# A gated mix of two attentions on one core: unit 14 normalised later, and the output projection's loads in two tiles a block

## The chip, the cores and the metric

The kernel runs on one core of a Trainium2 chip. A core has TensorE (matmuls), VectorE, ScalarE and GpSimd, each with its own queue of instructions that it works off in order; SyncE, whose queue here issues nearly all DMAs; and 16 DMA engines. The metric is device time of one execution in microseconds, the median of several runs.

## The reference

The input x has 2048 rows of 448. Two attentions with 16 heads of 28 columns read it, each with its own weights, and a gate mixes their outputs row by row:

```
g   = sigmoid(sum(x * gate_w))
q,k,v = x @ wqkv                           # for A and for B
A:  8 keys at distances 0, 2, .. 14 behind each row, softmax, times v
B:  all 2048 keys, softmax, times v
out = g * (a @ A_wo) + (1 - g) * (b @ B_wo)
```

The kernel puts g and 1 − g on the two attention outputs ahead of the projection. The projection is then one product: 2048 rows by 896 columns (448 of A, 448 of B) with the two stacked output weights.

## The kernel before, in words

**Numbers.** The matrices that go through TensorE in the projection are split in two parts, a rounded one (hi) and the rest (lo); each product is three matmuls, hi·hi, hi·lo, lo·hi. A split is one rounding copy, usually on ScalarE, and one subtraction on VectorE or GpSimd.

**Attention B** is cut in 16 units: u = 4·g + b is the group g of four heads with the block b of 512 query rows. A unit has 16 steps, one for each 128 keys; steps are counted through, 0 to 255, and the last unit, 15, is steps 240 to 255. In a step TensorE makes four score tiles (line 980), ScalarE two exponentials of 128x1024 (line 985), and TensorE adds the weighted sum of the step before into the accumulator `av` (line 946). While unit u runs, the scores of unit u + 1 are also made once for their row maxima; in unit 15 there is nothing left of that. Attention A runs beside it on GpSimd and VectorE; when its last output is stored, `a_done` is called, in step 240 here.

**Hooks.** Other work is hung into steps: `at(pos, st, f)` puts f into the program at a place of step st. "pre" is ahead of the step's scores, "dve" and "act" after them, "end" behind the weighted sum. A hook only sets the place in the order in which each engine's queue is filled. Within its queue an instruction starts as soon as its data are there.

**Normalising a unit** after its last step, with f its following unit's first step: `fin_copy` copies the accumulator with its row of sums (ScalarE, line 850); `fin_sum` stores the sums to DRAM (855); `fin_sum2` reads them back 16 to a partition (859); `fin_inv` inverts them and multiplies by 1 − g (863, 864); `fin_spread` stores that (868); `fin_spread2` reads it back, each head's row onto 32 partitions, four DMAs (873); `fin_on` multiplies on GpSimd (879); `fin_hi` rounds on ScalarE (883); `fin_lo` subtracts on GpSimd (887); `fin_store` stores both parts to DRAM, eight DMAs. The list `l` in the main loop gives the steps, counted from f. For unit 14 f is 240.

**The output projection.** Its 16 tiles j are of 128 rows; four tiles make a block b of 512 rows. A tile is seven pieces of the 896 columns, each three matmuls (line 832): 21 matmuls of 128x448. For each block the seven pieces are loaded: `op_load_a(b, k)`, k 0 to 3, loads A's output raw (one DMA, line 802, tall 128 rows, the last 64), which `op_split` splits (line 808 for block 0 on VectorE, 810 on ScalarE for the others, and 811 on VectorE); `op_load_b(b, k)` loads B's stored hi and lo (two DMAs, line 99, the helper `dma_r`). So a block is twelve loads. The tiles of blocks b and b + 1 have separate buffers. Raw pieces, unit outputs and results share one ring of eight buffers (`mtile`).

Block 0's loads are hung into steps by `a_done`. Tile 0's first nine matmuls are in step 255 between the last two weighted sums, and the rest of it follows the last weighted sum. `op_tile(j, behind)` is one tile of the projection: while block b is multiplied, it loads and splits block b + 1. `behind` is one step of unit 15's normalising for each of tiles 0 to 6: the sum in tile 0, the store in tile 6. Then `op_out` takes the tile out of its accumulator (two accumulators in turn; even tiles on ScalarE, line 843, odd ones on VectorE, line 841) and stores it (844). In SyncE's queue a tile's loads stand behind the result of the tile before, and ahead of what `behind` issues.

Of the kernel before, what the change touches and what calls it, by code (L numbers as in the profile page):

```python
# [20 lines left out]
NU = NG * NB  # L21
# [4 lines left out]
def gated_mix_kernel(ctx: ExitStack, tc: tile.TileContext, xT, xn, gw, wA, wB, woAB, out):  # L26
    nc = tc.nc
# [70 lines left out]
    def dma_r(dst, src):  # L98
        nc.sync.dma_start(dst.bitcast(F32), src.bitcast(F32))  # L99
# [112 lines left out]
    with tc.tile_pool(name="xp", bufs=1) as xp, tc.tile_pool(name="wp", bufs=2) as wp:  # L212
# [243 lines left out]
        for n, t in enumerate(tiles):  # L456
# [4 lines left out]
            for w in splits:  # L461
                i, k = (n - splits[w][0]) * splits[w][1], splits[w][1]
# [60 lines left out]
    def at(pos, st, f):  # L523
        hooks.setdefault((st, pos), []).append(f)
# [46 lines left out]
    def mtile(name):  # L571
        return pm.tile([128, 512], F32, tag="M", name=name)
# [185 lines left out]
    OP0 = NJ * (NU - 2)  # L758
# [19 lines left out]
    def a_done(st):  # L778
        adone.append(st)
        assert st < OP0 + 24, st  # L780
        actx.close()
        oP["2"] = ctx.enter_context(tc.tile_pool(name="wop2", bufs=2))
        for k in range(4):
            at("end", st + 1 + k, lambda k=k: (op_load_a(0, k), op_load_b(0, k)))
            at("dve", st + 4 + k, lambda k=k: op_split(0, k, nc.vector.tensor_copy))

    for k in range(7):
        at("pre", WO_AT + k, lambda k=k: raw_wo(k))
# [4 lines left out]
    def oa_tiles(b):  # L793
        if b not in oaT:
            oaT[b] = [[oP["2"].tile([128, 512], F32R, tag=f"oa{p}{k}", name=f"oa{p}{k}") for p in ("hi", "lo")]
                      for k in range(3)]
        return oaT[b] + [[t[0:64] for t in on_tiles(b)[0]]]

    def op_load_a(b, k):
        n = 128 if k < 3 else 64  # L800
        raws[b, k] = mtile("oar")[0:n]
        nc.sync.dma_start(raws[b, k], oa_scr[128 * k:128 * k + n, 512 * b:512 * b + 512])

    def op_split(b, k, rounded=None):
        raw = raws.pop((b, k))
        hi, lo = oa_tiles(b)[k]
        if rounded:
            rounded(hi, raw)
        else:
            nc.scalar.activation(hi, raw, AF.Copy)  # L810
        nc.vector.tensor_tensor(out=lo, in0=raw, in1=hi.bitcast(F32), op=ALU.subtract)

    def on_tiles(b):
        if b not in onT:
            onT[b] = [[oP["2"].tile([128, 512], F32R, tag=f"on{p}{k}", name=f"on{p}{k}") for p in ("hi", "lo")]
                      for k in range(4)]
        return onT[b]

    def op_load_b(b, k, rows=128):
        r0, p0 = (0, 64) if k == 0 else (128 * k - 64, 0)  # L820
        n = 64 if k == 0 else rows
        for t, src in zip(on_tiles(b)[k], (on_hi, on_lo)):
            dma_r(t[p0:p0 + n], src[r0:r0 + n, 512 * b:512 * b + 512])
# [3 lines left out]
    def op_mm(j, bank, ks, first=False, last=False):  # L827
        b, jj = divmod(j, 4)
        for k in ks:
            for i, (a, c) in enumerate(TERMS):  # L830
                src = (oaT[b][k] if k < 3 else onT[b][k - 3])[a][:, 128 * jj:128 * jj + 128]
                writes(bank, nc.tensor.matmul(bank[:, :D], src, wo[c][k],  # L832
                                              start=(first and k == ks[0] and i == 0),
                                              stop=(last and k == ks[-1] and i == 2)))

    def op_out(j, bank, eng=0):
        t = mtile("res")

        c = D // 2 if j == NJ - 1 else 0
        if eng:  # L840
            reads(bank, nc.vector.tensor_copy(t[:, c:D], bank[:, c:D]))
        if c or not eng:
            reads(bank, nc.scalar.activation(t[:, :c or D], bank[:, :c or D], AF.Copy))
        nc.sync.dma_start(out.rearrange("(p j) c -> p j c", j=NJ)[:, j, :], t[:, :D])
# [3 lines left out]
    def fin_copy(u):  # L848
        t = mp.tile([128, 512], F32, name="osb")
        nc.scalar.activation(t, av, AF.Copy)  # L850
        fin["o"] = t


    def fin_sum(u):
        nc.sync.dma_start(rs_scr[0][u].rearrange("(h c) -> h c", h=4), fin["o"][DH::32, :])

    def fin_sum2(u):
        fin["s"] = sp.tile([128, 16], F32, name="fsum")
        nc.sync.dma_start(fin["s"], rs_scr[0][u].rearrange("(p i) -> p i", i=16))

    def fin_inv(u):
        r = sp.tile([128, 16], F32, name="finv")
        nc.vector.reciprocal(r, fin["s"])
        nc.gpsimd.tensor_tensor(out=r, in0=r, in1=og[:, u % NB, :], op=ALU.mult)
        fin["rec"] = r

    def fin_spread(u):
        nc.sync.dma_start(rs_scr[1][u].rearrange("(p i) -> p i", i=16), fin["rec"])

    def fin_spread2(u):  # L870
        fin["r"] = mp.tile([128, 512], F32, name="rbc")
        for h in range(4):
            nc.sync.dma_start(fin["r"][32 * h:32 * h + 32, :],
                                rs_scr[1][u][512 * h:512 * h + 512].rearrange("(o c) -> o c", o=1).to_broadcast(
                                    [32, 512]))
# [5 lines left out]
    def fin_hi(u):  # L881
        fin["hi"] = mtile("onhi").bitcast(F32R)
        nc.scalar.activation(fin["hi"], fin["on"], AF.Copy)
# [5 lines left out]
    def fin_store(u):  # L889
        g, b = divmod(u, NB)  # L890
        for dst, t in ((on_hi, fin["hi"]), (on_lo, fin["lo"])):
            for h in range(4):
                r = 112 * g + DH * h
                dma_r(dst[r:r + DH, 512 * b:512 * b + 512], t[32 * h:32 * h + DH])

    def pool_time(f, *x):
        late["pool"] += 1.25
        f(*x)
# [6 lines left out]

    for u in range(NU - 1):
        f = NJ * (u + 1)
        l = {NU - 3: (1, 2, 5, 6, 9, 12, 13, 15), NU - 2: (1, 2, 5, 6, 8, 10, 10, 12)}.get(
            u, (1, 3, 6, 8, 12, 15, 16, 19))
        at("pre", f + 1, lambda u=u: fin_copy(u))  # L910
        at("end", f + l[0], lambda u=u: fin_sum(u))
        at("end", f + l[1], lambda u=u: fin_sum2(u))
        at("dve", f + l[2], lambda u=u: fin_inv(u))
        at("end", f + l[2], lambda u=u: fin_spread(u))
        at("end", f + l[3], lambda u=u: fin_spread2(u))
        at("end", f + l[4], lambda u=u: pool_time(fin_on, u, fin["r"]))
        at("pre", f + l[5], lambda u=u: fin_hi(u))
        at("end", f + l[6], lambda u=u: pool_time(fin_lo, u, nc.gpsimd))
        at("end", f + l[7], lambda u=u: fin_store(u))
# [4 lines left out]
    def op_tile(j, behind):  # L924
        bank = accs[j % 2]
        b, k = divmod(j, 4)
        if j:
            op_mm(j, bank, (0, 1), first=True)
        if b < 3:
            op_load_a(b + 1, k)  # L930
            op_load_b(b + 1, k)
            if k:
                op_split(b + 1, k - 1)
        for f in behind:
            f()
        op_mm(j, bank, (2, 3, 4, 5, 6) if j else (3, 4, 5, 6), last=True)
        if b < 3 and k == 3:
            op_split(b + 1, 3)
        op_out(j, bank, j % 2)

    prev = None
# [53 lines left out]
    for u in range(NU):  # L995
        g, b = divmod(u, NB)
        for kt in range(NJ):
            st = NJ * u + kt
# [7 lines left out]
            if not adone and not any(lists.values()) and st > stored[0]:  # L1006
                a_done(st)
# [40 lines left out]
    for j in range(NJ):  # L1048
        op_tile(j, steps[j] if j < len(steps) else ())
# [25 lines left out]
```

## Time and profile before

| | us |
|---|---|
| median of 3 runs | 918.8 (918.25 to 919.15) |
| the profiled execution | 919.04 |
| its span on the core | 917.2 |
| TensorE busy in the span | 900.8 (98%) |
| VectorE, ScalarE, GpSimd busy | 734.7, 646.9, 640.1 |
| DMA bytes, mean rate | 105.04 MB, 115 GB/s |

The span is what the profile shows of the execution; the 1.8 us between it and the execution's time lie around it. Lines of a profile name the engine, the line of the kernel, the operation and its tiles as out<-in; "PEld" is TensorE's weight load, "SPq" SyncE's queue, "PEclk" the clock granted to TensorE, in tenths of full speed. In answers in order of time a line starts with its start and its duration, and what stands in brackets is the engine's idle time before it and what ended it. Ends of matmuls are modelled, so that consecutive ones overlap in the listing.

### The profile page before, as it was taken

How to read it: one execution, taken by the hardware profiler on the slowest of the kernel's cores; microseconds unless marked ns; L12 is line 12 of the kernel's file. 1: busy time of each engine (PE TensorE's matmuls, PEld its weight loads, DVE VectorE, ACT ScalarE, POOL GpSimd, SP SyncE). 2: the span in 40 equal slices, each digit the busy share in tenths (PEclk: the TensorE clock that was granted, in tenths of full speed). 3: DMA queues.
4: the chain of work that ended last, by engine and by line, in shares of the span. 5: the costliest groups of instructions: out<-in, count | busy, mean ns of one | idle time of the engine just before them, and what ended most of it. 6: DMA issues, size and time to landing. Idle time of an engine off the chain costs nothing.

```text
span 917.2 us, 20553 instructions
## 1 busy us (share of the span) xinstructions
PE 900.8 (98%) x8326; PEld 541.5 (59%) x8326; DVE 734.7 (80%) x954; ACT 646.9 (71%) x777; POOL 640.1 (70%) x507
## 2 busy tenths in 40 slices
PE   9999999999999999999999999999999999979988
PEld 6799999999944444444444444444444444325977
DVE  6488999999979999999999999999999998320211
ACT  7356434343388899888888898888889888975210
POOL 2489846464469689999999998999996988110100
PEclk9999999999999999999999999999999999998999
DMA  9877402559363231325144235232212212452872
GB/s 270 293 239 196 144 13 82 151 128 127 83 242 104 78 105 45 93 53 169 45 124 119 40 105 132 48 97 84 61 40 85 55 35 55 122 146 69 226 198 79
DMA packets 116758, 105.04 MB, mean 115 GB/s; under 512 B 77192, under 2 KB 84744, under 8 KB 115880
## 3 DMA queue, kind: packets, MB, share of 16 engines
q1 hardware_dynamic: 116520, 103.47, 41.7%
q8 instruction: 65, 1.06, 0.5%
q10 hardware_dynamic: 144, 0.26, 0.1%
q14 instruction: 29, 0.24, 0.1%
HBM read 62.72 MB, written 40.96 MB: 113 GB/s over the span
## 4 chain that ended last, share of the span: by engine, by line
PE 90%; DMA 4%; SPq 3%; ACT 2%; issue 1%; DVE 0%; POOL 0%; ACTq 0%; POOLq 0%
PE T L980 29%; PE av L946 26%; PE r L304 15%; PE T L832 6%; PE r L299 6%; PE r L142 4%; PE T L142 4%; SPq L99 1%; ACT P L985 1%; DMA oar<-oa_scr 1%; DMA onlo<-on_lo 1%; DMA rs<-finv 1%; DMA onhi<-on_hi 1%; SPq L682 1%; DMA raw<-in_wB 0%
## 5 line engine op out<-in xcount | busy, mean ns | idle before, releaser
L985 ACT ACTIVATE P<-T 128x1024 f32<-128x1024 f32 x512 | 497.1, 1025 | 62.2 <-PE T L980 60.8
L148 DVE TENSOR_REDUCE MX<-T 128x1 f32<-128x512 f32 x470 | 442.1, 954 | 34.0 <-PE T L142 14.4
L946 PE MATMUL av<-P,V 128*32 128x512 f32 x2048 | 274.4, 608 | 0.9 <-ACT osb L850 0.9
L980 PEld LDWEIGHTS T<-QH,KH 30*128 30x128 f32 x1024 | 93.0, 182 | 238.9 <-ACT P L985 204.1
L980 PE MATMUL T<-QH,KH 30*128 30x512 f32 x1024 | 214.9, 491 | 5.8 <-ACT P L985 5.8
L142 PE MATMUL T<-KH,QP 28*128 28x512 f32 x704 | 220.3, 456 | 0.1
L164 DVE TENSOR_REDUCE MX<-r 128x2 f32<-128x1024 f32 x160 | 192.1, 1222 | 25.0 <-PE r L142 23.0
L980 PE MATMUL T<-QH,KL 28*128 28x512 f32 x1024 | 188.4, 397 | 0.0
L980 PE MATMUL T<-QL,KH 28*128 28x512 f32 x1024 | 187.0, 396 | 0.0
L609 POOL TENSOR_TENSOR prod<-qt,kt 128x896 f32<-128x896 f32 x64 | 135.3, 2115 | 5.0 <-DMA kt<-a_scr 5.0
L367 ACT ACTIVATE raw<-r 128x896 f32<-128x896 f32 (+1 forms) x64 | 58.9, 920 | 97.2 <-PE r L304 94.2
L670 POOL TENSOR_TENSOR oat<-oat,prod 128x896 f32<-128x896 f32 x48 | 101.2, 2108 | 2.0
L142 PEld LDWEIGHTS T<-KH,QP 28*128 28x128 f32 x704 | 86.1, 182 | 27.2 <-ACT P L985 17.6
L368 POOL TENSOR_TENSOR ast<-raw 128x448 f32<-128x448 f32 x48 | 55.4, 1153 | 58.2 <-ACT raw L367 45.5
L665 POOL TENSOR_TENSOR prod<-vt,L 128x896 f32<-128x896 f32 x56 | 95.3, 1702 | 0.2
L980 PEld LDWEIGHTS T<-QH,KL 28*128 28x128 f32 x1024 | 94.2, 184 | 0.9
L980 PEld LDWEIGHTS T<-QL,KH 28*128 28x128 f32 x1024 | 94.6, 186 | 0.0
L946 PEld LDWEIGHTS av<-P,V 128*32 128x32 f32 x2048 | 40.5, 108 | 79.2 <-issue 66.5
L304 PE MATMUL r<-wh,xh 64*128 64x448 f32 (+1 forms) x512 | 83.1, 363 | 0.0
L142 PE MATMUL r<-KH,QP 64*128 64x512 f32 x320 | 80.9, 393 | 1.0 <-DMA KH<-qk_hi 1.0
L304 PE MATMUL r<-wh,xl 64*128 64x448 f32 (+1 forms) x384 | 70.4, 364 | 0.0
L614 POOL TENSOR_TENSOR prod<-prod 128x448 f32<-128x448 f32 x64 | 65.6, 1024 | 5.0
(112 smaller groups left out, 1080.4 us busy)
## 6 DMA issues: line engine op xcount, KB each, us to landing
a_scr<-ast SPq DMA_DIRECT2D x24, 448.0 KB
qk_hi<-qkh SPq DMA_DIRECT2D x24, 256.0 KB
qk_lo<-qkh SPq DMA_DIRECT2D x24, 256.0 KB
rbc<-rs SPq DMA_DIRECT2D x64, 64.0 KB
QP<-qk_hi SPq DMA_DIRECT2D x64, 56.0 KB
KL<-qk_lo SPq DMA_DIRECT2D x16, 224.0 KB
QH<-qk_hi SPq DMA_DIRECT2D x64, 56.0 KB
QL<-qk_lo SPq DMA_DIRECT2D x64, 56.0 KB
```

The lines of the kernel that those rows point to most:

```text
L142: nc.tensor.matmul(bank, qhis[u][h % 2][r, 128 * qs:128 * qs + 128], KH[u // NB % 3][r, 512 * kc:512 * kc + 512], start=True, stop=True)
L148: i = nc.vector.tensor_reduce(MX[:, n % NMX:n % NMX + k], bank, axis=X, op=ALU.max)
L164: nc.vector.tensor_reduce(m, PM[k], axis=X, op=ALU.max)
L304: nc.tensor.matmul(bank[:, 0:cols], x, ws[c][rows, k, 0:cols], start=first, stop=last)
L367: nc.scalar.activation(raw[:, :, 0:cols], PJ[n % 2][:, :, 0:cols], AF.Copy)
L609: nc.gpsimd.tensor_tensor(out=p, in0=qt[c], in1=kvt["k", c % 2][:, HALO - DIL * w:HALO - DIL * w + NJ, :], op=ALU.mult)
L614: nc.gpsimd.tensor_tensor(out=lo, in0=lo, in1=hi, op=ALU.add)
L665: nc.gpsimd.tensor_tensor(out=dst.rearrange("p j (h d) -> p j h d", d=DH), in0=kvt["v", c % 2][:, HALO - DIL * w:HALO - DIL * w + NJ, :].r ...
L670: nc.gpsimd.tensor_tensor(out=ows[c % 2][:, :, 0:56] if w == W - 1 else oat[c], in0=oat[c], in1=oat[c, w], op=ALU.add)
L946: nc.tensor.matmul(av[32 * h:32 * h + 32, :], V[:, kt, 4 * g + h, :], tiles_[h], start=(kt == 0), stop=(kt == NJ - 1), skip_group_check=True)
L980: nc.tensor.matmul(bank[a], (KH[g % 3], KH[g % 3], KL[g % 2])[t][r, ks], (qh, ql, qh)[t][r, :], start=(t == 0), stop=(t == 2))
L985: e = nc.scalar.activation(p, one if a == "2" else mine, AF.Exp, scale=SCALE).ins
```

## The change

Three things are changed, and no instruction is added or removed.

1. Unit 14's `fin_on`, `fin_hi`, `fin_lo` and `fin_store` go from steps 248, 250, 250 and 252 to 252, 255, 255 and 255.
2. Block 0's loads go from the ends of steps 241, 242, 243 and 244 to 247, 249, 251 and 253 (`OP0 + 23` is 247), and their splits from 244 to 247 to 249, 251, 253 and 255.
3. Blocks 1 to 3: a block's four pieces are loaded two and two in the first two tiles of the block ahead, instead of one in each tile. The splits of two pieces stand one tile after their loads, so in the second and third tile, instead of one tile behind with the last one after the fourth tile's matmuls.

```diff
         for k in range(4):
-            at("end", st + 1 + k, lambda k=k: (op_load_a(0, k), op_load_b(0, k)))
-            at("dve", st + 4 + k, lambda k=k: op_split(0, k, nc.vector.tensor_copy))
+            at("end", max(st, OP0 + 23) + 2 * k, lambda k=k: (op_load_a(0, k), op_load_b(0, k)))
+            at("dve", max(st, OP0 + 23) + 2 * k + 2, lambda k=k: op_split(0, k, nc.vector.tensor_copy))
...
         f = NJ * (u + 1)
-        l = {NU - 3: (1, 2, 5, 6, 9, 12, 13, 15), NU - 2: (1, 2, 5, 6, 8, 10, 10, 12)}.get(
+        l = {NU - 3: (1, 2, 5, 6, 9, 12, 13, 15), NU - 2: (1, 2, 5, 6, 12, 15, 15, 15)}.get(
             u, (1, 3, 6, 8, 12, 15, 16, 19))
...
             op_mm(j, bank, (0, 1), first=True)
-        if b < 3:
-            op_load_a(b + 1, k)
-            op_load_b(b + 1, k)
-            if k:
-                op_split(b + 1, k - 1)
+        for i in (2 * k, 2 * k + 1) if b < 3 else ():
+            if i < 4:
+                op_load_a(b + 1, i)
+                op_load_b(b + 1, i)
+            if 2 <= i < 6:
+                op_split(b + 1, i - 2)
         for f in behind:
             f()
         op_mm(j, bank, (2, 3, 4, 5, 6) if j else (3, 4, 5, 6), last=True)
-        if b < 3 and k == 3:
-            op_split(b + 1, 3)
         op_out(j, bank, j % 2)
```

## The prediction

> **What bounds the kernel now.** I read the page first, then the waits of TensorE over the last 117 us, then the engines' instructions in order of time around the two waits that this view names. The page:
>
> ```profile
> span 917.2 us, 20553 instructions
> ...
> PE 900.8 (98%) x8326; PEld 541.5 (59%) x8326; DVE 734.7 (80%) x954; ACT 646.9 (71%) x777; POOL 640.1 (70%) x507
> ...
> PEclk9999999999999999999999999999999999998999
> ```
>
> TensorE is the bound. The idle part of its span, and the one slice with a lower granted clock, lie at the end, where all of the change lies. The waits of TensorE from 800 us on:
>
> ```profile
> PE T L980 <- ACT P L985: 5.6, 1, 5.6
> PE T L832 <- ACT onhi L810: 2.8, 1, 2.8
> ```
>
> The first is in the scores of the last unit, the second in the output projection. ScalarE around the first, in order of time (start, duration, instruction, idle before it):
>
> ```profile
> 787.36 0.63 ACT L883 ACTIVATE onhi<-on 128x512 fp32r<-128x512 f32 x1
> 787.88 3.81 ACT L985 ACTIVATE P<-T 128x1024 f32<-128x1024 f32 x4
> ...
> 810.28 7.84 ACT L985 ACTIVATE P<-T 128x1024 f32<-128x1024 f32 x8 [0.18 <-PE T L980]
> 823.70 0.63 ACT L883 ACTIVATE onhi<-on 128x512 fp32r<-128x512 f32 x1 [5.57 <-POOL on L879]
> ...
> 833.00 3.85 ACT L985 ACTIVATE P<-T 128x1024 f32<-128x1024 f32 x4 [0.64 <-PE T L980]
> 837.00 1.94 ACT L985 ACTIVATE P<-T 128x1024 f32<-128x1024 f32 x2 [0.15 <-PE T L980]
> ```
>
> At 818.12 (810.28 + 7.84) ScalarE is done with the exponentials of step 249, and next in its queue stands the rounding of unit 14 (L883, step 250). It waits 5.57 us for GpSimd's product (L879), and the exponentials behind it wait too; so TensorE starves. Why the product is late, in SyncE's queue (L855 sum, L859 sum read back, L868 reciprocals out, L873 spread over 32 rows, L802 and L99 loads and stores):
>
> ```profile
> 804.38 0.53 SPq L855 DMA_DIRECT2D rs<-osb  x1
> 805.01 0.38 SPq L802 DMA_DIRECT2D oar<-oa_scr  x1
> ...
> 806.72 0.52 SPq L859 DMA_DIRECT2D fsum<-rs  x1
> ...
> 813.32 0.32 SPq L868 DMA_DIRECT2D rs<-finv  x1
> 819.00 1.72 SPq L873 DMA_DIRECT2D rbc<-rs  x4
> 824.35 1.59 SPq L99 DMA_DIRECT2D on_hi<-onhi  x4
> ...
> 827.76 0.35 SPq L802 DMA_DIRECT2D oar<-oa_scr  x1
> ```
>
> Twelve loads of the first output block stand between the steps of unit 14's chain, and the 8 KB of reciprocals take 5.67 us from issue (813.32) to the next issue (819.00), behind the loads' bytes. For unit 13, with no such loads, the same pair stands 1.43 us apart:
>
> ```profile
> 774.14 0.35 SPq L868 DMA_DIRECT2D rs<-finv  x1
> 775.57 1.71 SPq L873 DMA_DIRECT2D rbc<-rs  x4
> ```
>
> The output projection is 16 tiles of 21 matmuls (12 on the first after the last unit). ScalarE evicts the even ones, and so marks their pace:
>
> ```profile
> 843.67 0.54 ACT L843 ACTIVATE res<-T 128x448 f32<-128x448 f32 x1 [1.97 <-PE T L832]
> ...
> 860.77 0.55 ACT L843 ACTIVATE res<-T 128x448 f32<-128x448 f32 x1 [3.15 <-PE T L832]
> ...
> 869.33 0.54 ACT L843 ACTIVATE res<-T 128x448 f32<-128x448 f32 x1 [2.12 <-PE T L832]
> ...
> 877.55 0.63 ACT L810 ACTIVATE onhi<-oar 64x512 fp32r<-64x512 f32 x1 [4.22 <-DMA oar<-oa_scr]
> 882.62 0.54 ACT L843 ACTIVATE res<-T 128x448 f32<-128x448 f32 x1 [4.43 <-PE T L832]
> ...
> 909.20 0.55 ACT L843 ACTIVATE res<-T 128x448 f32<-128x448 f32 x1 [7.96 <-PE T L832]
> ```
>
> An undisturbed pair of tiles takes 8.56 us (860.77 to 869.33), 4.28 a tile; the next pair takes 13.29. Tile 8 waits for the split of block 2's last piece (877.55), which waits for a load issued late, since unit 15's eight stores went ahead of it:
>
> ```profile
> 868.12 2.53 SPq L99 DMA_DIRECT2D on_hi<-onhi  x4
> 870.75 3.57 SPq L99 DMA_DIRECT2D on_lo<-onlo  x4
> 874.42 0.36 SPq L844 DMA_DIRECT2D out<-res  x1
> 874.84 0.46 SPq L802 DMA_DIRECT2D oar<-oa_scr  x1
> ```
>
> After both waits TensorE runs at half clock for a while, by the windows (span, length, busy time of each engine, granted clock, DMA share, GB/s):
>
> ```profile
> 828.00:830.00 2.00, 2.00 (x16) 0.84 (x12) 0.00 (x0) 0.51 (x1) 0.00 (x0) 0.50 0.53 124
> ...
> 880.00:882.00 2.00, 2.00 (x6) 1.77 (x6) 0.00 (x0) 0.00 (x0) 0.00 (x0) 0.50 0.71 203
> ```
>
> **The change part by part.**
>
> (a) Unit 14's rounding goes from the head of step 250 to the head of step 255. The matmuls of the weighted sum mark TensorE's steps (249, 254, 255):
>
> ```profile
> 818.18 1.07 PE L946 MATMUL av<-P,V 128*32 128x512 f32 x8
> ...
> 836.90 1.07 PE L946 MATMUL av<-P,V 128*32 128x512 f32 x8
> ...
> 839.92 1.06 PE L946 MATMUL av<-P,V 128*32 128x512 f32 x8
> ```
>
> From step 249 to 254 it takes 836.90 − 818.18 = 18.72 us. Eight exponentials in 7.84 us are 1.96 a step; with the idle 0.18 of the same row and TensorE's hand-over I take 2.00. Five steps are then 10.0, and the stall with its half clock is worth 8.7 us (8.9 at 1.96, 8.2 at 2.1). The rounding does not vanish: it now stands ahead of the exponentials of step 255 and costs ScalarE 0.52 us (787.36 to 787.88). These end at 838.94 (837.00 + 1.94), and the sum that needs them starts at 839.92 because the first nine output matmuls stand ahead of it; that cover of 0.98 us takes the 0.52. Without it, +0.5.
>
> (b) Is the product there by step 255? With the loads behind the spread, the chain on SyncE is sum, read back, reciprocals, spread. With unit 13's 1.43 us, the reciprocals go out at about 810 and the spread at about 811.5, so the product ends near 816. ScalarE asks for it at about 818.1 + 5 × 2.0 = 828.1. Even as late as now it would end in time:
>
> ```profile
> 822.40 1.26 POOL L879 TENSOR_TENSOR on<-osb,rbc 128x512 f32<-128x512 f32 x1 [11.90 <-DMA rbc<-rs]
> ```
>
> So 823.7 against 828.1. GpSimd has nothing behind it then; the tail of the chain (rounding, low part, eight stores) ends some 4 us later in the sequence of steps.
>
> (c) The first block's loads. SyncE is not paced by steps but only by data, so "two steps apart" means that they go out as soon as the spread is issued: about 813.2. Now the first is issued at 805.01 and the last piece is rounded here:
>
> ```profile
> 817.60 0.42 DVE L808 CAST onhi<-oar 64x512 fp32r<-64x512 f32 x1 [0.98 <-DMA oar<-oa_scr]
> 818.05 0.68 DVE L811 TENSOR_TENSOR onlo<-oar,onhi 64x512 fp32r<-64x512 f32 x1
> ```
>
> That is 12.6 us for a block of 2.75 MB (twelve loads by the code: nine of 128x512 f32, 256 KB, and three of 64x512, 128 KB). So they would be in by about 826, or by 833.3 if the spread went out no earlier than now (819.00 + 1.72 + 12.6). The first nine output matmuls come 1.0 after step 254's sum, at about 829.2 by (a), and the rest at 832.2. Cost nothing, with 3 to 6 us of cover; at the other end, 833.3 plus 1.1 for its split (0.42 and 0.68) is 2.2 us of waiting, plus a half-clock stretch.
>
> (d) Block 1's first loads now stand behind unit 14's stores, which wait for the low part: rounding 828.0 to 828.6, GpSimd's subtraction to 829.9 (estimated at the 1.26 of its product of the same shape), the last four stores to about 831.6 (four took 1.59). They were issued at 827.76, 13 us ahead of the projection; now about with its start, and two tiles' worth together. They are wanted at tile 4, 12 matmuls (12/21 of 4.28) and three tiles later: 2.4 + 12.8 = 15.2 us. The 12.6 us of a block fit with 2 to 3 us left. Unit 15's sum on SyncE stands behind six loads instead of three: about +1.5 us on a chain whose result is first read at tile 12.
>
> (e) Blocks 2 and 3: six loads in each of the first two tiles, none in the others. All of block 2's loads are now issued in tiles 4 and 5, ahead of unit 15's stores in tile 6; block 3's in tiles 8 and 9 instead of 8 to 11. So both late pieces go. Over tiles 0 to 14 the loss is (909.20 − 843.67) − 7 × 8.56 = 5.6 us, and all of it goes (nearest bound below: 4.7, the pair 6 to 8 alone). The number of instructions and bytes is the same.
>
> What the bursts cost: 2.75 MB in two tiles (8.56 us) would be 321 GB/s. The rates shown are these:
>
> ```profile
> 805.00:817.60 12.60, 12.60 (x125) 4.83 (x126) 4.24 (x9) 12.27 (x15) 0.22 (x1) 1.00 0.79 221
> ...
> 844.00:857.00 13.00, 13.00 (x66) 11.99 (x65) 2.95 (x5) 2.55 (x6) 0.22 (x1) 1.00 0.79 205
> ```
>
> At 221 GB/s a block lasts into its third tile. There ScalarE has the last two splits ahead of that tile's eviction: loads from 0.9 to 13.5 us after the block's first tile began, split 0.63, eviction 0.54: 14.7. The accumulator is wanted again at 4 × 4.28 = 17.1. I take nothing, since 2.4 us remain.
>
> Sum: 8.7 + 5.6 = 14.3 us. The profiled execution took 919.04 us (span 917.2), 0.24 above the median of 918.8. 919.04 − 14.3 = 904.7, or 904.5 against the median.
>
> [...] The row first: the wait named in the projection is 2.8 us, and the clock is 0.50 in 880 to 882. [...] The 5.6 are read off the tiles' pace, whatever the cause; the half clock after such a wait costs 4.73 − 2.8 = 1.9 us (4.73 being 13.29 − 8.56).
>
> **The rivals.**
> 1. The first stall goes, the projection's does not: the doubled loads only move the late piece (a split behind a burst, at tile 4, 8 or 12). For it: 321 GB/s wanted, 221 shown. Against: no load is behind unit 15's stores any more. 919.04 − 8.7 = 910.3, 910.1 on the median.
> 2. The first block comes late at the hand-over, (c)'s other end: 2.2 us plus 1.9 for the half clock = 4.1, 908.6. For it: a spread as late as 819. Against: what made it late now stands behind it.
> 3. Slower: ScalarE's queue in each block's third tile. From 15.0 us a block (2.4 over the 12.6) the late splits hold the eviction and TensorE waits for the accumulator, three times. With 1.9 us of half clock each time, all 14.3 us are eaten at 4.8 a block, that is by loads of 17.9 us or 154 GB/s. At 146 GB/s (18.9 us) it would be 904.5 + 3 × 5.8 = 921.9. Against: 205 and 221 shown with the same traffic.
> 4. It does not do what it says: since SyncE is paced by data, only order counts, and if the chain's 5.67 us came from something other than the loads, the reciprocals stay slow. Then the moved rounding alone still clears the stall, see (b): this ends as rival 2, and no change would need both to fail.
>
> **How the numbers follow.** Forecast (both stalls gone) 0.73; rival 1 0.12; rivals 2 and 4 0.09; rival 3 0.04; no change 0.02. The predicted time is 904.5. Its own range is 903.4 (1.96 us a step, 904.3, less the 0.9 by which the runs shown differ) to 906 (8.2 at 2.1 us a step, 905.0, and the same 0.9); rivals 1 and 2 stretch the range to 910.2. About 0.2% (1.8 us; the runs shown lie within 0.9) is what a measurement of this kernel can tell from no change. Faster 0.94, same 0.02, slower 0.04.
>
> **What would show it.** ScalarE's L883 of unit 14 with no wait, near 828, and TensorE's steps at 2.0 us up to the last; L850 of the last unit near 832.4 instead of 841.10; the reciprocals' gap near 1.4 us instead of 5.67, with all twelve loads behind the spread; clock 1.00 from 820 on; evictions of even tiles 8.56 us apart throughout. The forecast is wrong if L832 waits for a split (L810, L811 or L808), or if an eviction (L843, L841) stands behind a split that waits for its load.

## The result and the profile after

The changed kernel takes 907.26 us (median of 4 runs, 906.29 to 907.92) against 918.97 (4 runs, 918.25 to 920.69): a ratio of 0.9869, 95% interval 0.9852 to 0.9886. It is faster by 11.7 us; 14.3 had been forecast. The profiled execution took 906.91 us. Its page, beside the page shown of before:

```profile
span 905.1 us, 20549 instructions
...
PE 896.3 (99%) x8326; PEld 539.4 (60%) x8326; DVE 734.6 (81%) x954; ACT 646.9 (71%) x777; POOL 640.7 (71%) x507
...
PEclk9999999999999999999999999999999999999999
```

The slice with the lower clock is gone. The four instructions fewer than before are none of those counted above: each engine's count is the same. The view of what TensorE waited for, over the same last stretch (line numbers behind the change are one lower than before: 945, 979, 984 for 946, 980, 985):

```profile
PE av L945 <- ACT osb L850: 0.9, 1, 0.9
PE T L832 <- ACT res L843: 0.6, 1, 0.6
```

Neither of the two waits is left; the 0.9 us behind L850 stood there before as well. A small new one is the last: L832 waits 0.6 us for an eviction. ScalarE in order of time, around the first:

```profile
819.63 9.93 ACT L984 ACTIVATE P<-T 128x1024 f32<-128x1024 f32 x10
829.44 0.63 ACT L883 ACTIVATE onhi<-on 128x512 fp32r<-128x512 f32 x1
829.96 1.94 ACT L984 ACTIVATE P<-T 128x1024 f32<-128x1024 f32 x2
833.81 0.60 ACT L850 ACTIVATE osb<-av 128x512 f32<-128x512 f32 x1 [1.91 <-issue]
```

Ten exponentials run through where the stall had been, and unit 14's rounding stands at the head of step 255 without a wait. SyncE's queue, and GpSimd's product:

```profile
809.71 0.34 SPq L868 DMA_DIRECT2D rs<-finv  x1
811.14 1.72 SPq L873 DMA_DIRECT2D rbc<-rs  x4
812.95 0.37 SPq L802 DMA_DIRECT2D oar<-oa_scr  x1
...
833.52 1.42 SPq L802 DMA_DIRECT2D oar<-oa_scr  x1
```

```profile
814.84 1.29 POOL L879 TENSOR_TENSOR on<-osb,rbc 128x512 f32<-128x512 f32 x1 [5.15 <-ACT P L984]
```

The reciprocals go out at 809.71 and the spread 1.43 us later instead of 5.67; the loads follow at 812.95, and block 1's at 833.52.

Three marks divide each profile: unit 14's `fin_copy` (L850), the last unit's L850, and the last L843. All that is ahead of the first is the same in both kernels. The last column is TensorE's wait near tile 8 alone, with what it waited for; e1 and e3 have one at tile 4 too, which is told below. The experiments below are in the table too.

| profile | L850 of unit 14 at | to the last L850 | from there to the last L843 | wait near tile 8 |
|---|---|---|---|---|
| before | 798.87 | 42.23 | 72.80 | 2.84, L810 |
| before, again (b1, b2) | 800.36, 799.67 | 41.97, 41.69 | 71.57, 72.64 | 2.31, 2.54, L810 |
| changed | 800.21 | 33.60 | 68.02 | 0.55, L843 |
| changed, again (r, r2) | 801.99, 799.83 | 33.58, 33.60 | 67.46, 67.75 | none; 0.3, L843 |
| e1, unit 14 and first loads | 799.91 | 33.59 | 72.98 | 2.07, L810 |
| e2, projection's loads | 801.10 | 41.43 | 67.32 | none |
| e3, unit 14's steps | 800.45 | 33.61 | 71.42 | 1.84, L810 |
| e4, first loads | 801.59 | 33.86 | 72.19 | 1.83, L810 |
| e5, evictions first | 801.46 | 33.61 | 67.20 | none |
| e6, store behind loads | 800.93 | 33.62 | 67.97 | 0.21, L810 |
| e7, more bytes | 802.38 | 33.60 | 78.54 | see there |
| e8, all three | 799.16 | 33.81 | 67.25 | none |

### The profile page after: what moved, and what is told of

The parts are those of the page before. It is cut to its first block, busy times and chain, and to the rows that moved or that the text cites. A ratio compares the mean times of both kernels' runs of the same rounds, so it can differ in the third digit from the quotient of the medians.

```text
span 905.1 us, 20549 instructions
## 1 busy us (share of the span) xinstructions
PE 896.3 (99%) x8326; PEld 539.4 (60%) x8326; DVE 734.6 (81%) x954; ACT 646.9 (71%) x777; POOL 640.7 (71%) x507
## 4 chain that ended last, share of the span: by engine, by line
PE 93%; DMA 3%; ACT 2%; SPq 1%; DVE 0%; issue 0%; ACTq 0%
PE T L979 30%; PE av L945 27%; PE r L304 15%; PE T L832 6%; PE r L299 6%; PE r L142 4%; PE T L142 4%; ACT P L984 1%; DMA V<-in_xT 1%; DMA onlo<-on_lo 1%; DMA out<-res 0%; DMA qk_hi<-qkh 0%; DMA KH<-qk_hi 0%; SPq L99 0%; ACT KH L775 0%
## 5 line engine op out<-in xcount | busy, mean ns | idle before, releaser
L670 POOL TENSOR_TENSOR oat<-oat,prod 128x896 f32<-128x896 f32 x48 | 101.3, 2111 | 2.0
```

Of the source, the lines that this page charges most:

```text
L670: nc.gpsimd.tensor_tensor(out=ows[c % 2][:, :, 0:56] if w == W - 1 else oat[c], in0=oat[c], in1=oat[c, w], op=ALU.add)
```

## The experiments

**The parts of the change, one at a time.** e1 has unit 14's later steps and the first block's later loads, e2 the projection's part alone, and e3 and e4 divide e1 again.

```diff
# e1 = both of these on the kernel before; e3 = the second alone; e4 = the first alone
-            at("end", st + 1 + k, lambda k=k: (op_load_a(0, k), op_load_b(0, k)))
-            at("dve", st + 4 + k, lambda k=k: op_split(0, k, nc.vector.tensor_copy))
+            at("end", max(st, OP0 + 23) + 2 * k, lambda k=k: (op_load_a(0, k), op_load_b(0, k)))
+            at("dve", max(st, OP0 + 23) + 2 * k + 2, lambda k=k: op_split(0, k, nc.vector.tensor_copy))
...
-        ... NU - 2: (1, 2, 5, 6, 8, 10, 10, 12)
+        ... NU - 2: (1, 2, 5, 6, 12, 15, 15, 15)
# e2 = only the edit of op_tile
```

> Unit 14's later steps and the first block's later loads; the projection's loads as before. My theory: the two stalls are separate and add up, so this has the 8.7 us of the first one alone: 910.2, with the last unit's L850 some 8.7 us earlier relative to unit 14's L850, and the wait of L832 on L810 near tile 8 still there with about 5 us lost over the tiles. Rival (the parts depend on each other, the projection's loads collide with what is moved behind the step 255): less than 6 us gained, 913 or more.

> The projection's loads in two tiles and the splits a tile behind, nothing else. My theory: the stall at step 250 stays (about 5.6 us of waiting, half clock after it), and the projection gains the 4.8 us that the changed kernel's tiles show (of the 5.6 forecast): 914.2. Rival (the late piece only moves, or the doubled loads need the emptier queue of the other parts): 917 or more.

> Unit 14's later steps alone; the first block's loads stay between the steps of its chain. By point (b) of the prediction the product is there at 823.7 even with the reciprocals held up for some 5.7 us, and ScalarE asks for it at about 828: no stall, 8.7 us gained, 910.2. Rival (the loads' collision is what costs, and the wait only moves to step 255): a wait of ScalarE L883 of over 1 us at step 255, and under 7 us gained, 912 or more.

> The first block's later loads alone; unit 14 is rounded at step 250 as before. If the loads' bytes are what held up the reciprocals, these take about 1.4 us instead of 5.7, the product ends some 2 to 3 us before ScalarE asks for it at step 250, and the stall goes by this alone: 8.7 us gained, 910.2. Rival (the reciprocals are slow for another reason, or 1.4 us is only reached when the rounding is later too): the wait of L883 stays at 3 us or more, 914 to 919.

| | median us | ratio to before, 95% interval |
|---|---|---|
| before (same chip, 11 runs) | 920.17 | |
| e1 | 912.07 (909.6 to 914.13) | 0.9913, 0.9882 to 0.9943 |
| e2 | 914.81 (914.37 to 916.39) | 0.9947, 0.9932 to 0.9961 |
| e3 | 911.49 (910.66 to 912.43) | 0.9908, 0.9882 to 0.9934 |
| e4 | 912.13 (910.11 to 913.16) | 0.9912, 0.9884 to 0.9939 |

e1 gains 8.1 us and e2 5.4. Together that is 13.5, a little above the 11.7 to 12.2 of the whole change, and within the two intervals: the two stalls are separate. What TensorE waits for in e1, from 800 us on, and in e2:

```profile
PE T L832 <- ACT onhi L810: 3.0, 2, 2.1
PE av L946 <- ACT osb L850: 0.9, 1, 0.9
```

```profile
PE T L979 <- ACT P L984: 5.5, 1, 5.5
PE av L945 <- ACT osb L850: 0.9, 1, 0.9
```

Each keeps the wait that its part leaves alone. e1 has one more, which the kernel before does not have: of its two waits on L810, 2.07 us stands near tile 8 and this one at tile 4, for block 1's last piece:

```profile
851.60 0.47 PE L832 MATMUL T<-KH,onhi 128*128 128x448 f32 x1 [0.92 <-ACT onhi L810]
```

With unit 14's store so late, block 1's first load goes out at 833.23 here, against 827.76 before. e3 has the same wait with 0.68 us. e6 below, whose program is the same as e1's up to tile 6, does not have it, so it comes in some executions only. The changed kernel, with its doubled loads, has it in none of its three profiles.

e3 and e4 both take the first stall away, and by different means. In e3 the loads still collide: SyncE's queue, GpSimd's product, and ScalarE's rounding are

```profile
814.95 0.35 SPq L868 DMA_DIRECT2D rs<-finv  x1
820.44 1.83 SPq L873 DMA_DIRECT2D rbc<-rs  x4
```

```profile
823.97 1.28 POOL L879 TENSOR_TENSOR on<-osb,rbc 128x512 f32<-128x512 f32 x1 [12.11 <-DMA rbc<-rs]
```

```profile
829.69 0.63 ACT L883 ACTIVATE onhi<-on 128x512 fp32r<-128x512 f32 x1
```

The reciprocals are as slow as before (5.49 us from issue to the next), the product ends at 825.25, and it is asked for 4.4 us later. In e4 the rounding stays at step 250 and the loads are out of the way. There the same rows read:

```profile
811.62 0.34 SPq L868 DMA_DIRECT2D rs<-finv  x1
813.05 1.72 SPq L873 DMA_DIRECT2D rbc<-rs  x4
```

```profile
816.57 1.29 POOL L879 TENSOR_TENSOR on<-osb,rbc 128x512 f32<-128x512 f32 x1 [4.97 <-DMA rbc<-rs]
```

```profile
820.74 0.63 ACT L883 ACTIVATE onhi<-on 128x512 fp32r<-128x512 f32 x1
```

1.43 us for the reciprocals, the product done at 817.86, asked for at 820.74. That settles what held up the reciprocals: the first block's loads. It also shows that the change removed this stall twice over. The table gives the small difference, one profile each: 33.86 in e4 against 33.61 in e3, 0.25 of the 0.52 us that the rounding takes on ScalarE.

**The changed kernel again, and the kernel before again.**

> The changed kernel once more, beside the others on one chip. My theory: what the forecast of 904.5 missed is about 0.8 us at tile 8 and, for the rest, the spread of the work ahead of the changed stage, which is the same in all kernels. So from unit 14's L850 to the last unit's L850 it takes 33.6 us again, from there to the last L843 68.0, and unit 14's L850 itself falls anywhere between 798.5 and 802. Rival (the change itself slows what is ahead of it): L850 of unit 14 later than in the kernels that keep the old order.

> The changed kernel a third time: 33.6 us from unit 14's L850 to the last unit's, and 67.4 to 68.1 from there to the last L843, according to whether the eviction of tile 6 stands behind its splits long enough to be waited for.

> The kernel before, profiled once more, to see how typical the execution was from which the forecast took its terms. My theory: the work ahead of unit 14's L850 takes longer than the 798.9 us shown (800 to 802, as in the other runs), so that the forecast started from a fast one; from there to the last unit's L850 42.2 us again; and the projection varies by 1 to 2 us (71 to 73 from L850 to the last L843), since the half clock after the wait at tile 8 came in two of three runs with such a wait. Rival (the first profile was typical, 798.9 and 72.8): then the gain in the medians should have been near 14.

> The same once more, for the spread: 800 to 802 ahead of unit 14's L850, 42.2 to the last unit's, 71 to 73 to the last L843; with half clock after the wait at tile 8 where it is nearer 73.

The changed kernel had 907.97 us (906.77 to 908.16), before on the same chip 920.12 (13 runs): 0.9869, 0.9853 to 0.9884. The single runs gave 919.24 and 919.28 for before and 906.26 for the changed kernel. By the table the last unit's stretch repeats within 0.02 us in the changed kernel and varies by 0.54 in the one before. TensorE ran at half clock after the wait at tile 8 in all three profiles of before (0.50, 0.51 and 0.50 in the slowest window of 2 us), so that its coming alone does not explain their 71.57 to 72.80. The part ahead of unit 14's L850 varies from 798.87 to 802.38 over the fourteen profiles, with no order by kernel: the execution from which the forecast took its terms was the quickest there, by 0.3 us to the next (e8). The means are 799.6 for before (three profiles) and 800.7 for the changed kernel (three). That 1.0 lies within the spread; that the change slows what is ahead of it is neither shown nor excluded.

**The 0.6 us wait at tile 8.** e5 is the changed kernel with the splits behind the tile's eviction:

```diff
-            if 2 <= i < 6:
-                op_split(b + 1, i - 2)
...
         op_out(j, bank, j % 2)
+        for i in (2 * k, 2 * k + 1) if b < 3 else ():
+            if 2 <= i < 6:
+                op_split(b + 1, i - 2)
```

> The changed kernel with the two splits of a tile moved behind that tile's eviction, so that no eviction stands behind a split that waits for its load. My theory: the 0.6 us wait of L832 on L843 at tile 8 was tile 6's eviction held up by the split ahead of it in ScalarE's queue; it goes, even tiles are 8.56 us apart throughout, and the time from the last unit's L850 to the last L843 falls from 68.0 to 67.2: 0.8 us less than the changed kernel. Rival (the split itself, now later, is waited for, or the wait is the load's): 68.0 or more, with a wait of L832 on L810 or L811.

ScalarE in the changed kernel, tiles 6 and 8:

```profile
865.71 0.63 ACT L810 ACTIVATE onhi<-oar 64x512 fp32r<-64x512 f32 x1 [1.64 <-DMA on_hi<-onhi]
866.25 0.52 ACT L843 ACTIVATE res<-T 128x448 f32<-128x448 f32 x1
871.42 0.54 ACT L843 ACTIVATE res<-T 128x448 f32<-128x448 f32 x1 [4.65 <-PE T L832]
```

Four tiles after tile 4 (853.49) tile 8 is evicted 17.93 us later, where 17.12 is undisturbed. The row at 865.71 names one of unit 15's stores as what released the split. By the code the split reads only its load, which was issued at 858.59, and waits for no store; that it waited for the load is therefore read from the code, and is not what this row says. The same split in tiles 2 and 10 (847.04 and 881.19) names its load. In e5:

```profile
862.62 0.63 ACT L810 ACTIVATE oahi<-oar 128x512 fp32r<-128x512 f32 x1 [2.98 <-DMA oar<-oa_scr]
865.97 0.54 ACT L843 ACTIVATE res<-T 128x448 f32<-128x448 f32 x1 [2.72 <-POOL onlo L887]
```

The eviction now stands ahead of the splits, and TensorE has no wait of 0.1 us or more from 830 us to the end; the stretch is 67.20 against 68.02, 67.46 and 67.75. But tile 6 is still evicted late, 11.23 us after tile 4 (854.74): there ScalarE was released by GpSimd's low part of unit 15 (L887). So "8.56 throughout" was a miss; that this wait is for a buffer of the shared ring is likely from the code and was not tested. In time e5 has 906.86 us (905.53 to 908.01), 0.9859, 0.9841 to 0.9877: not told apart from the changed kernel.

e8 adds to this an earlier rounding of unit 14:

```diff
# on e5
-        ... NU - 2: (1, 2, 5, 6, 12, 15, 15, 15)
+        ... NU - 2: (1, 2, 5, 6, 10, 12, 12, 13)
```

> The evictions ahead of the splits, and unit 14 rounded at step 252 and stored at 253 instead of 255, so that block 1's loads go out about 5 us earlier. My theory: nothing is left in TensorE's way in either order, so it equals the kernel with the evictions ahead: 33.6 us from unit 14's L850 to the last unit's and 67.2 to the last L843, 906 to 907 in all, within the spread of that kernel and about 1 us under the changed one. Rival (the rounding at step 252 costs its 0.5 us of ScalarE, which only step 255's place hides): 34.1 us for the first of the two.

905.96 us (905.29 to 908.21), 0.9878, 0.9857 to 0.99, with before at 918.31 (7 runs) on that chip. It is the lowest median, and not told apart from e5 or the changed kernel. Its 33.81 for the last unit show 0.2 of the rounding's 0.5 us, which neither theory had.

**What made block 2's last piece late.** e6 is e1 with unit 15's store one tile later, so that it stands behind that tile's load; no loads are doubled.

```diff
# on e1
-             [lambda: fin_lo(u, nc.gpsimd), lambda: fin_store(u)])
+             [lambda: fin_lo(u, nc.gpsimd)], [lambda: fin_store(u)])
```

> Unit 14's and the first block's later steps, the projection's loads as before, one in each tile; only unit 15's store goes from tile 6 to tile 7, where it stands behind the load of block 2's last piece. If it was the stores ahead of that load that made it late, the wait at tile 8 goes, with its half clock, without any doubled loads: about 4 us less than the first experiment from the last unit's L850 to the last L843 (73.0 there), so 69 or less, 907 in all. Rival (one load in each tile is too late by itself): a wait of L832 on L810 of 1.5 us or more near tile 8 stays, 72 or more.

909.16 us (907.59 to 910.03), 0.9883, 0.9865 to 0.99; 907 had been expected. From the last L850 to the last L843 it has 67.97 where e1 has 72.98. Block 2's last piece is asked for 29.24 us after that L850 (863.79) instead of 34.52 (868.02), and TensorE's only wait in the projection's tiles is

```profile
PE T L832 <- ACT onhi L810: 0.2, 1, 0.2
```

So the order of the stores and one load in SyncE's queue was the cause of the wait at tile 8: the wait fell from 2.07 to 0.21 us, and tiles 6 to 8 took 9.32 us instead of e1's 12.22, 2.9 less. Of the 5.0 between the two profiles 1.4 arose at tiles 2 to 4, ahead of anything that the edit touches, by e1's wait at tile 4. The medians, 912.07 and 909.16, differ by 2.9 as well. The changed kernel had 907.97 beside e6, 1.2 less, and the two intervals overlap: whether one store moved by a tile gives all that the doubled loads give is not settled.

**The slower rival's price.** e7 is the changed kernel with one more load of 256 KB for each piece of blocks 1 to 3:

```diff
+    def extra(b, k):
+        for n, p in enumerate((on_hi,)):
+            t = oP["2"].tile([128, 512], F32, tag=f"ex{k}{n}", name=f"ex{k}{n}", bufs=1)
+            r = 128 * k if k < 3 else 320
+            nc.sync.dma_start(t, p.bitcast(F32)[r:r + 128, 512 * b - 512:512 * b])
...
                 op_load_b(b + 1, i)
+                extra(b + 1, i)
```

> The changed kernel with one more load of 256 KB for each piece of blocks 1 to 3, into tiles that nothing reads: 3.80 MB a block instead of 2.75. It tests the slower rival's price. By that rival's own arithmetic (221 GB/s, 12.6 us becomes 17.4; 2.4 us over its point of 15.0, and 1.9 of half clock, three blocks) it is 12.9 us slower than the changed kernel, some 920. My theory after the result: the changed kernel's windows show 297 and 315 GB/s in the bursts, so that a block of 3.80 MB with its results takes some 14 to 15 us: evictions later by 2 to 4 us, waits of TensorE of 0 to 2.5 us a block, and 2 to 6 us in all.

916.21 us (914.41 to 920.3), 0.9962, 0.9946 to 0.9979: 8.2 us above the changed kernel's 907.97. Its profile is of a run near the upper end (919.79). What TensorE waits for, and ScalarE in block 3's third tile (six lines have been added, so L838, L847, L849 are the matmul and the two evictions):

```profile
PE T L838 <- ACT res L849: 6.2, 3, 2.2
PE T L838 <- DVE res L847: 1.0, 1, 1.0
```

```profile
894.04 0.63 ACT L810 ACTIVATE onhi<-oar 64x512 fp32r<-64x512 f32 x1 [3.76 <-DMA oar<-oa_scr]
894.58 0.52 ACT L849 ACTIVATE res<-T 128x448 f32<-128x448 f32 x1
```

This is the rival's mechanism to the letter, an eviction behind a split that waits for its load, and a matmul that waits for the accumulator. The rate in the bursts, by the windows of e7 (the first two rows) and of the changed kernel:

```profile
846.00:854.00 8.00, 6.08 (x30) 5.12 (x29) 2.20 (x4) 1.69 (x3) 0.00 (x0) 1.00 0.89 304
...
886.00:894.00 8.00, 7.10 (x35) 6.20 (x33) 1.92 (x3) 1.23 (x2) 0.00 (x0) 1.00 0.99 323
```

```profile
858.00:866.00 8.00, 8.00 (x41) 7.29 (x39) 2.61 (x4) 2.08 (x4) 1.30 (x1) 1.00 1.00 315
...
874.00:882.00 8.00, 8.00 (x41) 7.38 (x40) 2.54 (x5) 2.08 (x4) 0.00 (x0) 1.00 0.95 297
```

The measured 8.2 lies between my 2 to 6, reckoned with these peaks, and the 12.9 of the rival's 221 GB/s. Both were off. In the bursts the DMA engines move more than 221 (297 to 323 in these windows), which makes the rival's price too high. Why mine was too low was not tested; the four waits of the profile, 1.92, 0.96, 2.21 and 2.05 us, alone add up to 7.1, and the granted clock was lower after the first (0.57 in 854 to 858) and the last (0.70 in 896 to 900).

## Why the prediction was right, and where a size was off

**The sum.** Forecast 8.7 + 5.6 = 14.3 and 904.5; measured 907.26, within the range and outside the forecast's own 903.4 to 906. Of the two profiles compared, the last unit's stretch fell by 42.23 − 33.60 = 8.63 and the projection's by 72.80 − 68.02 = 4.78, 13.4 in all, while the part ahead was 1.34 longer: 12.1 between the two executions (919.04 and 906.91; the last digits are rounding and the end).

**(a) Right**, 8.63 for 8.7 (8.4 between the means of three profiles each). With the later start of this execution, 1.34 us, taken off, the rounding stands at 828.1 (forecast 828) and the last L850 at 832.5 (832.4). The rounding behind the nine output matmuls costs the least there: 33.60 with it at step 255, 33.86 and 33.81 with it at steps 250 and 252, one profile each.

**(b) Right on both sides.** e3 has the product at 825.25 against 829.69; the prediction, from the other execution, had 823.7 against 828.1: the same 4.4 us of room. The loads as the cause of the 5.67 us are shown by e4. The prediction did not see that moving the loads alone would do: with its own numbers (product at 816, rounding asked for at 818.1) that could have been said.

**(c) Right.** The first block's last piece was rounded on VectorE at

```profile
824.69 0.42 DVE L808 CAST onhi<-oar 64x512 fp32r<-64x512 f32 x1 [1.58 <-DMA oar<-oa_scr]
```

11.7 us after its first load (12.6 forecast) and 5.9 us before the nine output matmuls (830.60).

**(d), (e): the mechanism right, one term mis-sized.** Block 1's doubled loads fitted as forecast: the first went out at 833.52, the split of the last piece ended at 848.38, and the matmul that needs it began at 850.83, 2.4 us later (2 to 3 had been reckoned). The late pieces of the kernel before went, and e6 shows that block 2's was late for the reason given. But "I take nothing, since 2.4 us remain" was 0.8 off in the profiled run: the eviction of tile 6 began at 866.25, 4.2 us later than two undisturbed tiles after tile 4's (853.49 + 8.56), and tile 8 lost 17.93 − 17.12 = 0.8. The sum for a block's third tile (loads 12.6 us from 0.9 after the block's start) left out that block 2's loads start late: tile 4 began at

```profile
849.01 0.57 PE L832 MATMUL T<-KH,oahi 128*128 128x448 f32 x2
```

and its first load went out 3.6 us after that, not 0.9. In tile 4 the loads stand in SyncE's queue behind unit 15's spread, which waits for the reciprocals, and these stand on VectorE directly behind block 1's last split:

```profile
847.70 0.68 DVE L811 TENSOR_TENSOR onlo<-oar,onhi 64x512 fp32r<-64x512 f32 x1 [2.67 <-ACT onhi L810]
848.34 0.25 DVE L863 RECIPROCAL finv<-fsum 128x16 f32<-128x16 f32 x1
```

The spread, a result and block 2's first load then go out at

```profile
850.37 1.71 SPq L873 DMA_DIRECT2D rbc<-rs  x4
852.18 0.37 SPq L844 DMA_DIRECT2D out<-res  x1
852.60 0.42 SPq L802 DMA_DIRECT2D oar<-oa_scr  x1
```

and the last split begins 13.1 us after that load (865.71). So the time of the loads was right within 0.5 us, and their start was 2.7 us off, which is more than the 2.4 us that were to cover it. The other profiles with doubled loads go the same way: the first load 3.6 us behind the tile's start gives a wait of 0.28 us (r2), 3.2 us (r) and 2.7 us (e2, with unit 14's store as early as before) give none.

One sign that the prediction named as wrong for it did appear: an eviction behind a split that waits for its load. It was so in the third tile of each of the first three blocks, in which the next block is split: tiles 2, 6 and 10 were evicted 11.2, 12.8 and 10.3 us after the tile before them on ScalarE, not 8.56. At tiles 2 and 10 the spare time took it, at tile 6 it did not quite.

**What the forecast could not read from one profile.** The two changed stretches took 115.0 us in the profile shown, and 114.3 as the mean of three; changed, they took 101.3 as a mean (three profiles). So 13.0 is the gain of these stages, 1.3 under the forecast: 0.5 for the loss at tile 8 (67.7 against e5's 67.2) and 0.7 since both stretches were longer in the profile shown of before than the mean of three (its wait at tile 8 was the longest). The medians differ by 11.7 and 12.2, and a single run of the changed kernel lay 12.1 under the third median of before; the remaining 1 is of the size of the spread of the part ahead, and its cause stays open.

**The rivals.** Rival 1 (projection unchanged) is refuted by e2, rival 4 by e4. Rival 2 did not come. Rival 3 came in miniature in the changed kernel and in full in e7, at a price between two estimates.

## What to carry to other kernels

SyncE's queue was paced by data and not by the place in the program: here loads written two steps, some 4 us, apart went out 1.6 us apart (812.95, 814.55). What mattered here was which few small, awaited transfers stood behind which large ones: moving the large ones behind was worth the whole first stall (e4: 33.86 us in the last unit's stretch against 42.23). Where two edits each remove the same stall, one of them is free for something else, so try them apart. Moving work later also moves what stands behind it: unit 14's later store brought block 1's loads close enough to their use for a wait at tile 4 in e1 (0.92 us) and e3 (0.68). And an eviction should not stand in a queue behind work that waits for a load: the doubled loads were harmless here with some 0.5 us lost, and cost 8.2 more when a block's bytes grew by 38%.

## What the runs showed of the hardware that had not been expected

**Half clock after waits of 1.8 to 2.8 us, and not after each.** TensorE waited 2.84, 2.31, 2.54, 2.07 and 1.83 us near tile 8 in before, b1, b2, e1 and e4, and the granted clock fell to about 0.50 behind all five; in e3 it waited 1.84 us and the clock stayed at 1.00. The windows of e4 and of e3 (span, length, busy time of each engine, granted clock, DMA share, GB/s):

```profile
872.00:874.00 2.00, 1.95 (x7) 1.46 (x8) 1.13 (x2) 0.00 (x0) 0.00 (x0) 0.83 0.44 145
874.00:876.00 2.00, 2.00 (x6) 1.79 (x6) 0.00 (x0) 0.00 (x0) 0.00 (x0) 0.50 0.70 208
```

```profile
872.00:874.00 2.00, 1.96 (x10) 1.72 (x10) 0.64 (x2) 0.00 (x0) 0.00 (x0) 1.00 0.47 168
874.00:876.00 2.00, 2.00 (x12) 1.84 (x11) 0.00 (x0) 0.55 (x1) 0.00 (x0) 1.00 0.66 158
```

Tiles 6 to 8 took 12.22 us in e4 and 10.96 in e3 for the same wait; the difference, 1.3 us, is my estimate of what the half clock cost. The forecast had 1.9 for it, taken from one run as the pair's whole excess less the wait; e3's 0.56 of excess beyond its wait, with no half clock, belongs to neither. In e7 a wait of 1.92 us was followed by a mean clock of 0.57 (854 to 858 us) and one of 2.05 by 0.70 (896 to 900); behind one of 2.21 the clock stayed at 1.00 (876 to 880). Why a wait of the same length was followed by half clock in one run and not in another was not shown.

**A small transfer behind large ones.** 8 KB of reciprocals took 1.43 us from issue to the next issue with none of the block's loads ahead (e4), and 5.49 to 5.67 behind twelve loads of 2.75 MB in all (e3, before).
